# Another order for SP's loads and transposes in a fused attention and MLP kernel, with one matmul block moved on TensorE

## The chip, the cores and the metric

The kernel runs on one core of a Trainium2 chip. The metric is the device time of one execution in microseconds (us). Before the change it is 216.46 us, the median of four runs (215.32 to 217.26).

## The reference

Decayed linear attention over 4 batches, 8 heads, 768 positions and a head dimension of 64, in blocks of 64 positions with a running state, and then a layer norm with an MLP (512 to 2048 to 512) and a residual:

```python
for b in range(nb):                      # blocks of 64 positions
    intra = einsum('bhic,bhjc->bhij', qb, kb) * Dmask[None]
    intra = einsum('bhij,bhjd->bhid', intra, vb)
    inter = einsum('bhid,bhde->bhie', qb * lam_pow[None], kv_state)
    out[:, :, sl] = intra + inter
    kv_state = lam_block * kv_state + einsum('bhsd,bhse->bhde', kb * rev_pow, vb)
...
mu = mean(x); var = mean((x - mu) ** 2)
xn = (x - mu) / sqrt(var + 1e-06) * g_ln
out = x + maximum(xn @ w_ch1, 0.0) @ w_ch2
```

## The kernel before

The 4 x 768 rows are cut into 12 units of 256 positions, called pairs here (two chunks of 128), numbered u = 0 to 11; u goes over the batches first and then along the sequence, so pairs 0 to 3 start their sequences with no state. For each pair the kernel loads k, q and v (`load_one`, `load_window`, `fill`; lines 64 to 93) in float32 on SP's queue; rescales them to bf16 (`in_k` L199, `in_q` L210, `in_v` L216, the last giving the tile vb, mostly on GpSimd, called POOL); turns k and q by DMA transposes on SP (`transpose_dma`, L231, kq^T; for pairs 0 to 2 on TensorE, L224); computes k^T v (`kv`, L281, or `kv64`, L346), updates the state (`new_state`: a sum on VectorE, L291, and a decay on POOL, L287, or for a first state on ScalarE, L306), computes scores (`scores`, L247) and masks them on VectorE (`mask`, L257), multiplies them with v (`av`, L393) and adds the part from the state (`inter`, L406). `norm` (L428 to L435) gives xc, `to_xT` turns it into x^T (a DMA transpose on SP, L451, from pair 2 on), and `mlp` multiplies with both weights (L484 with ReLU L487; L522 with the residual L543), and the result is stored by SP (L550).

The order is written out by hand and nothing reorders it: each engine and each queue takes its instructions in the order in which the Python code issues them. Lines 588 to 695 do so for pairs 0 and 1 and begin pairs 2 to 4. Here `m1s(m1a, c, lo, hi)` issues the first-layer groups of pair 0 on weight chunk c, half a chunk (8 matmuls) at a time, `kv(1)` is the k^T v of pair 1, and `behind(tile)` makes POOL wait for a load before it issues more. From then on a list `plan` holds one MLP step each (8 matmuls of L484, or 4 of L522), and `add(n, ...)` puts steps of the attention behind the plan's step n: `p0(u)` converts the inputs of pair u, `s1(u)` to `s4(u)` do its attention, `p4(u)` issues its x^T, `transpose_dma` its kq^T, `load_one` one of its loads. Pairs from 6 on have another layout of the loads and the states (`X1`, `X2`, `X`).

The input tiles kin, qin and vin have three buffers each, so that the load of pair u takes the buffer of pair u - 3; vb has four; the PSUM tiles of the scores, tag "sc", have two. In `s1` the order on VectorE is: sum of the first state, mask of the first score tile, sum of the second state (which reads the first state after POOL has decayed it), mask of the second score tile; `s2` writes the next scores into the same two PSUM tiles. `make_keep64` builds a mask on POOL and copies half of it on VectorE (L142).

Of the kernel before, what the change touches and what calls it, by code (L numbers as in the profile page):

```python
# [16 lines left out]
def kernel(  # L17
# [11 lines left out]
    nc = tc.nc  # L29
# [38 lines left out]
    def fill(got, name, u, hs):  # L68
        src = dict(k=k, q=q, v=v)[name]
        if u < LB:  # L70
            nc.sync.dma_start(got[:, hs], source(src, u, hs))  # L71
            return
        cc, b = divmod(u, B)
        for j in range(2):
            nc.sync.dma_start(got[:, hs, j * D:(j + 1) * D],
                              src[b, hs, cc * W + j * C:cc * W + (j + 1) * C, :].rearrange("h p d -> p h d"))

    def load_one(u, name):
        got = inp.tile([128, H, 2 * D], F32, tag=name + "in", name=name + "in")
        fill(got, name, u, slice(0, H))  # L80
        qkv_in.setdefault(u, {})[name] = got.rearrange("p h (j d) -> p h j d", j=2)

    def load_window(u, after_pool=False, parts=1):
        got = {name: inp.tile([128, H, 2 * D], F32, tag=name + "in", name=name + "in") for name in "kqv"}
        if after_pool:

            nc.gpsimd.memset(got["k"][:, 0, 0:1], 0.0)
        n = H // parts
        order = [(name, i) for i in range(parts) for name in "kq"] + [("v", i) for i in range(parts)]
        for name, i in order:  # L90
            hs = slice(i * n, (i + 1) * n)
            fill(got[name], name, u, hs)
        qkv_in[u] = {name: f.rearrange("p h (j d) -> p h j d", j=2) for name, f in got.items()}
# [88 lines left out]
    def open_window(u):  # L182
        kq = wk.tile([128, 2, NP, 2, 2, D], BF16, tag="kq", bufs=3, name="kq")
        vb = wk.tile([128, H, 2, D], BF16, tag="vb", bufs=4, name="vb")
        st[u] = dict(kq=kq, vb=vb)
        if u < XB:
            st[u]["kqT"] = wk.tile([128, 2, NP, 2, 128], BF16, tag="kqT", bufs=3, name="kqT")
# [7 lines left out]
    def in_k(u, eng, hs=ALL):  # L195
        src = qkv_in[u]["k"][:, hs].rearrange("p (a e) j d -> p a e j d", e=2)
        dst = part(0, st[u]["kq"], hs)
        for j in range(2):
            (eng.copy if eng is nc.scalar else eng.tensor_copy)(dst[:, :, :, j], src[:, :, :, j])  # L199

    def in_q(u, eng, hs=ALL):
        src = qkv_in[u]["q"][:, hs].rearrange("p (a e) j d -> p a e j d", e=2)
        dst = part(1, st[u]["kq"], hs)
        if u < LB:
            lq = lam_q[:, hs, :].rearrange("p (a e) j -> p a e j", e=2)
        else:
            lq = lam_p[:, 0:1, hs].rearrange("p j (a e) -> p a e j", e=2).to_broadcast([128, (hs.stop - hs.start) // 2, 2, 2])
        n = (hs.stop - hs.start) // 2
        for j in range(2):
            eng.tensor_tensor(dst[:, :, :, j], src[:, :, :, j],  # L210
                              lq[:, :, :, j:j + 1].to_broadcast([128, n, 2, D]), op=ALU.mult)

    def in_v(u, eng, hs=ALL):
        n = hs.stop - hs.start
        lv = lam_v[:, hs, :, None] if u < LB else lam_p[:, 1, hs, None, None]
        eng.tensor_tensor(st[u]["vb"][:, hs], qkv_in[u]["v"][:, hs], lv.to_broadcast([128, n, 2, D]), op=ALU.mult)  # L216
# [36 lines left out]
    def mask(u, hf, heads=(0, 1)):  # L253
        s = st[u]
        kp = keep.rearrange("p a b t -> p a (b t)")
        for e in heads:
            nc.vector.tensor_tensor(s[f"mA{hf}"][:, e], s[f"sc{hf}"][e],  # L257
                                    kp[:, None, :, :].to_broadcast([128, 2, 2, 128]), op=ALU.mult)
# [11 lines left out]
    def kv(u, tag="mm"):  # L270

        s = st[u]
        cc, b = divmod(u, B)
        n_ab = 2 if (cc + 1) * W < S else 1
        bufs = dict(mm=4, sc=2, po=1)[tag]
        pk = [ps.tile([128, 2, NP, D], F32, tag=f"po{ab}" if tag == "po" else tag, bufs=bufs, name=f"pk{ab}")[:, 0] for ab in range(n_ab)]
        for p in range(NP):
            for j in range(2):
                for e in range(2):
                    for ab in range(n_ab):  # L280
                        nc.tensor.matmul(pk[ab][half[e], p, :], lhsT=s["kq"][half[ab], 0, p, j, e],  # L281
                                         rhs=s["vb"][half[ab], 2 * p + e, j],
                                         start=(p == 0 and j == 0), stop=(p == NP - 1 and j == 1), skip_group_check=True)
        s["pk"] = pk
# [9 lines left out]
    def new_state(u, ab, eng):  # L294

        s = st[u]
        b = u % B
        if ab == 1 and len(s["pk"]) == 1:
            return
        old = state.get(b)  # L300
        if ab == 0:
            s["S"] = [(old, old)]
        Sn = wk.tile([128, NP, D], BF16, tag="S", bufs=12, name="Sn")
        if old is None and eng is nc.scalar:
            for p in range(NP):
                nc.scalar.activation(Sn[:, p], s["pk"][ab][:, p], ACT.Identity, scale=lam_s[:, p:p + 1])  # L306
        elif old is None:
            decay(nc.vector, Sn, s["pk"][ab])
        else:
            tmp = s.pop("tmp", None) or state_sum(u, ab)  # L310
            decay(eng, Sn, tmp)
        state[b] = Sn
        if ab == 0:
            s["S"].append((Sn, Sn))
# [143 lines left out]
    def rstd_of(u):  # L458
        s = st[u]
        std = wk.tile([128, 2], F32, tag="std", name="std")  # L460
        nc.scalar.activation(std, s["mv"][:, :, 1], ACT.Sqrt, bias=eps_t)
        rstd = xp.tile([128, 2], F32, tag="rstd", name="rstd")
        nc.vector.reciprocal(rstd, std)
        x_keep[u] = (s["x"], rstd)
# [173 lines left out]
    m1a, m2a = mlp(0)  # L638
    m1b, m2b = mlp(1)

    def m1s(f, c, lo=0, hi=2):
        n = f.count // NWC
        for u in range(c * n + lo * n // 2, c * n + hi * n // 2):
            f(u)
# [17 lines left out]
    mask(1, 0)  # L662
    mask(1, 1)
    m1s(m1a, 1, 0, 1)
    kv(1, "sc")
    new_state(1, 0, nc.scalar)
    m1s(m1a, 1, 1, 2)
    rstd_of(0)
    m1s(m1a, 2, 0, 1)
    av(1, (0, 1))  # L670
# [21 lines left out]
    load_w2(3)  # L692
    in_v(2, nc.gpsimd)
    load_window(3, after_pool=True)
    load_window(4)

    def p0(u, k_eng=None):
        open_window(u)
        in_k(u, k_eng or nc.gpsimd)
        in_q(u, nc.gpsimd)  # L700
        in_v(u, nc.gpsimd)

    def s0(u):
        kv(u, "po")
# [138 lines left out]
    def add(at, *steps):  # L843
        after.setdefault(at, []).extend(steps)
# [6 lines left out]
    add(8, (s0, 2))  # L851
    add(10, (s3, 2))
    add(12, (s4, 2), (p4, 2), (p0, 3, nc.vector), (transpose_dma, 3))
    for n, name in zip((14, 15, 16), "kqv"):
        add(n, (load_one, 5, name))
    add(15, (rstd_of, 2))
    add(17, (p0, 4))
    add(25, (s1, 3))
    add(25, (transpose_dma, 4))
    add(27, (s2, 3))  # L860
    add(28, (p0, 5))
    add(29, (s3, 3))
    add(30, (s4, 3), (p4, 3))
    for n, name in zip((30, 31, 32), "kqv"):
        add(n, (load_one, 6, name))
    add(34, (rstd_of, 3), (make_keep64,))
    add(37, (transpose_dma, 5))
    add(38, (s1, 4))
    add(39, (p0, 6))
# [57 lines left out]
```

## Time and profile before

| | |
|---|---|
| median of four runs | 216.46 us |
| profiled execution | 216.34 us, of which the span is 214.4 us |
| TensorE matmul (PE) busy | 202.3 us, 94% of the span |
| VectorE (DVE), ScalarE (ACT), GpSimd (POOL) busy | 104.3, 87.2, 79.6 us |
| DMA moved | 37.13 MB, mean 173 GB/s |
| SP's DMA queue (q1) | 32.38 MB, 72.0% of 16 engines' span |

A line of a timeline gives the start in us from the start of the span, the duration in us, engine, line of the kernel, operation, what is written and read, the count, and in brackets how long the engine stood idle before it and what ended that. A line of the waits gives who waited for whom, us in total, how many times, and the longest. A line of a DMA issue ends with the us from the start of the issue to the landing of the data.

### The profile page before, as it was taken

The numbers are of one execution on the slowest core, as the hardware profiler recorded it, in microseconds if no ns is written. First come the engines' busy times: TensorE is split into PE (matmuls) and PEld (weight loads), VectorE is DVE, ScalarE is ACT, GpSimd is POOL, SyncE is SP. The second block draws the span as 40 slices with busy tenths as digits, with TensorE's granted clock in tenths as the row PEclk, the third lists the DMA queues.
The fourth block names the chain that finished last, engine by engine and source line by source line (L and its number), as shares of the span: only waits on it lengthen the run. The fifth ranks groups of instructions, "written<-read, shape, count | busy, mean of one in ns | idle before, by whom it ended". The sixth has DMA issues, their size and how long they took to land.

```text
span 214.4 us, 6657 instructions
## 1 busy us (share of the span) xinstructions
PE 202.3 (94%) x2899; PEld 138.2 (64%) x2899; DVE 104.3 (49%) x225; ACT 87.2 (41%) x165; POOL 79.6 (37%) x111
## 2 busy tenths in 40 slices
PE   2988799999999999999999999999999999999992
PEld 0467688544684675585585685784784874866861
DVE  2688380559268436747347256174183292522011
ACT  3865669220352244055163162361470460731600
POOL 4646339119656173229019137056074020000000
PEclk9999999999999999999999999999999999999999
DMA  4999999999999899999799799998998411320303
GB/s 114 295 272 210 202 279 145 225 275 274 196 305 243 168 210 167 114 215 211 134 228 191 146 235 185 191 213 179 208 244 133 117 28 28 99 52 0 98 3 95
DMA packets 94142, 37.13 MB, mean 173 GB/s; under 512 B 68385, under 2 KB 91169, under 8 KB 94114
## 3 DMA queue, kind: packets, MB, share of 16 engines
q1 hardware_dynamic: 89584, 32.38, 72.0%
q0 software_dynamic: 4224, 4.19, 12.4%
q8 instruction: 22, 0.36, 0.7%
q10 hardware_dynamic: 306, 0.14, 0.3%
q14 instruction: 6, 0.05, 0.1%
HBM read 27.27 MB, written 6.29 MB: 157 GB/s over the span
## 4 chain that ended last, share of the span: by engine, by line
PE 82%; DMA 8%; DVE 4%; SPq 3%; POOL 1%; issue 0%; ACT 0%; DVEq 0%
PE pm L484 37%; PE pm L522 34%; DMA vin<-in_v_dram 6%; SPq L71 3%; PE pm2h L513 2%; DMA xT<-xc 2%; PE po L393 2%; PE po L406 1%; PE sc L247 1%; DVE kq L199 1%; DVE xc L435 1%; PE po L380 1%; PE pk L281 1%; DVE stats L430 1%; POOL vb L216 1%; PE sc L327 1%
## 5 line engine op out<-in xcount | busy, mean ns | idle before, releaser
L487 ACT ACTIVATE hT<-pm 128x512 bf16<-128x512 f32 x92 | 55.0, 601 | 89.3 <-PE pm L484 89.1
L484 PE MATMUL pm<-xT,w 128*128 128x256 bf16 x736 | 86.1, 273 | 1.4 <-DMA w<-in_moe_w_ch_dram 0.9
L522 PE MATMUL pm<-w,hT 128*128 128x512 bf16 x368 | 82.3, 379 | 0.0
L484 PEld LDWEIGHTS <-w 128*128 128x128 bf16 x736 | 70.0, 98 | 13.0 <-DMA w<-in_moe_w_ch_dram 1.1
L522 PEld LDWEIGHTS <-hT 128*128 128x128 bf16 x368 | 35.5, 98 | 40.0
L543 DVE SCALAR_TENSOR_TENSOR o<-pm,rstd,x 128x512 f32<-128x512 f32 x23 | 17.1, 748 | 41.6 <-PE pm L522 41.4
L287 POOL TENSOR_TENSOR Sn<-Stmp,lam_s 128x256 bf16<-128x256 f32 x16 | 9.8, 614 | 69.1 <-DVE Stmp L365 49.0
L435 DVE SCALAR_TENSOR_TENSOR xc<-po,mv,g_row 128x512 bf16<-128x512 f32 (+1 forms) x24 | 16.8, 706 | 1.8
L257 DVE TENSOR_TENSOR mA<-sc,keep 128x512 bf16<-128x512 f32 x20 | 13.1, 684 | 6.5 <-PE sc L247 6.4
L428 ACT COPY x<-po 128x512 f32<-128x512 f32 x18 | 9.9, 589 | 11.3 <-PE po L393 5.5
L430 DVE BATCH_NORM_STATS2 stats<-x 128x6 f32<-128x512 f32 x18 | 12.4, 687 | 4.0 <-ACT x L428 3.9
L417 DVE COPY seen<-po 128x8 f32<-128x8 f32 x18 | 2.3, 162 | 23.1 <-PE po L406 23.1
L216 POOL TENSOR_TENSOR vb<-vin,lam_v 128x1024 bf16<-128x1024 f32 (+1 forms) x7 | 11.7, 1683 | 4.7 <-DMA vin<-in_v_dram 3.7
L210 POOL TENSOR_TENSOR kq<-qin,lam_q 128x512 bf16<-128x512 f32 x10 | 10.3, 1045 | 6.9 <-DMA qin<-in_q_dram 6.9
L210 POOL TENSOR_TENSOR kq<-qin,lam_p 128x512 bf16<-128x512 f32 x12 | 12.3, 1044 | 0.7 <-DMA qin<-in_q_dram 0.7
L216 POOL TENSOR_TENSOR vb<-vin,lam_p 128x1024 bf16<-128x1024 f32 x6 | 11.4, 1897 | 1.4 <-DMA vin<-in_v_dram 1.2
L199 POOL CAST kq<-kin 128x512 bf16<-128x512 f32 (+1 forms) x18 | 10.5, 611 | 0.6 <-DMA kin<-in_k_dram 0.6
L333 DVE TENSOR_TENSOR mA<-sc,keep 128x512 bf16<-128x512 f32 x12 | 8.2, 681 | 1.4 <-PE sc L327 1.4
L406 PE MATMUL po<-Sn,kqT 64*64 64x64 bf16 x216 | 7.4, 199 | 0.0
L224 PE MATMUL tp<-ident,kq 128*128 128x128 bf16 x48 | 6.1, 276 | 0.4 <-ACT kq L199 0.2
L224 PEld LDWEIGHTS <-kq 128*128 128x128 bf16 x48 | 4.1, 120 | 3.6 <-DVE kq L199 1.5
L406 PEld LDWEIGHTS <-kqT 64*64 64x64 bf16 x304 | 5.2, 108 | 1.5 <-issue 1.5
(98 smaller groups left out, 147.6 us busy)
## 6 DMA issues: line engine op xcount, KB each, us to landing
out_dram<-o SPq DMA_DIRECT2D x22, 256.0 KB, 4.9
w<-in_moe_w_ch_dram POOLq DMA_DIRECT2D x8, 512.0 KB, 10.2
kin<-in_k_dram SPq DMA_DIRECT2D x14, 256.0 KB, 3.7
qin<-in_q_dram SPq DMA_DIRECT2D x14, 256.0 KB, 4.9
vin<-in_v_dram SPq DMA_DIRECT2D x14, 256.0 KB, 5.7
kin<-in_k_dram SPq DMA_DIRECT2D x5, 512.0 KB, 8.1
qin<-in_q_dram SPq DMA_DIRECT2D x5, 512.0 KB, 8.6
vin<-in_v_dram SPq DMA_DIRECT2D x5, 512.0 KB, 6.9
```

Of the source, the lines that this page charges most:

```text
L199: (eng.copy if eng is nc.scalar else eng.tensor_copy)(dst[:, :, :, j], src[:, :, :, j])
L210: eng.tensor_tensor(dst[:, :, :, j], src[:, :, :, j], lq[:, :, :, j:j + 1].to_broadcast([128, n, 2, D]), op=ALU.mult)
L216: eng.tensor_tensor(st[u]["vb"][:, hs], qkv_in[u]["v"][:, hs], lv.to_broadcast([128, n, 2, D]), op=ALU.mult)
L224: nc.tensor.transpose(tp[:, i, j, :], s["kq"][:, a, p, j], ident)
L257: nc.vector.tensor_tensor(s[f"mA{hf}"][:, e], s[f"sc{hf}"][e], kp[:, None, :, :].to_broadcast([128, 2, 2, 128]), op=ALU.mult)
L406: nc.tensor.matmul(s["po"][ab][half[jq], 2 * p + e, :], lhsT=qT[half[e], p, jq, half[ab]], rhs=s["S"][ab][jq][half[e], p, :], start=False, ...
L430: nc.vector.bn_stats(stats, po if early else x)
L435: nc.vector.scalar_tensor_tensor(xc[:, sl], in0=po[:, sl], scalar=mv[:, 0:1], in1=g_row[:, sl], op0=ALU.subtract, op1=ALU.mult)
L484: nc.tensor.matmul(pm[:, b, :], lhsT=w1[n // W2K][:, kk, (n % W2K) * 128:(n % W2K + 1) * 128], rhs=xT_of[g][:, kk, 0:N], start=(b == 0 and ...
L487: nc.scalar.activation(hT[:, u * NB:(u + 1) * NB, 0:N], pm, ACT.Relu)
L522: nc.tensor.matmul(acc[i], lhsT=hT[:, kk, i * 128:(i + 1) * 128], rhs=w2[kk // W2K][:, kk % W2K, :], start=(kk == 0), stop=(kk == KB - 1))
L543: nc.vector.scalar_tensor_tensor(o[:, ab], in0=a, scalar=rstd[:, ab:ab + 1], in1=x[:, ab], op0=ALU.mult, op1=ALU.add)
```

## The change

Four things move; no operation is added or taken away.

1. `kv(1)` and the first state of pair 1 go behind the second half of the chunk-1 groups of pair 0's MLP.
2. The v load of pair 4 goes from ahead of pair 2's x^T to behind plan step 17, and that of pairs 5 and 6 to behind steps 31 and 38; the k and q loads of pair 5 go from 14 and 15 to 18 and 19, those of pair 6 from 30 and 31 to 32 and 33.
3. `in_v` of pairs 4, 5 and 6 leaves `p0` and stands at steps 26, 43 and 48; `p0(5)` goes from 28 to 31.
4. `transpose_dma` of pair 4 goes from 25 to 17.

```diff
     m1s(m1a, 1, 0, 1)
+    m1s(m1a, 1, 1, 2)
     kv(1, "sc")
     new_state(1, 0, nc.scalar)
-    m1s(m1a, 1, 1, 2)
     rstd_of(0)
...
     load_window(3, after_pool=True)
-    load_window(4)
+    load_one(4, "k")
+    load_one(4, "q")
 
     def p0(u, k_eng=None):
         open_window(u)
         in_k(u, k_eng or nc.gpsimd)
         in_q(u, nc.gpsimd)
-        in_v(u, nc.gpsimd)
+        if u not in (4, 5, 6):
+            in_v(u, nc.gpsimd)
...
-    for n, name in zip((14, 15, 16), "kqv"):
+    for n, name in zip((18, 19, 31), "kqv"):
         add(n, (load_one, 5, name))
     add(15, (rstd_of, 2))
-    add(17, (p0, 4))
+    add(17, (load_one, 4, "v"), (p0, 4), (transpose_dma, 4))
     add(25, (s1, 3))
-    add(25, (transpose_dma, 4))
     add(27, (s2, 3))
-    add(28, (p0, 5))
+    add(31, (p0, 5))
     add(29, (s3, 3))
     add(30, (s4, 3), (p4, 3))
-    for n, name in zip((30, 31, 32), "kqv"):
+    for n, name in zip((32, 33, 38), "kqv"):
         add(n, (load_one, 6, name))
     add(34, (rstd_of, 3), (make_keep64,))
+    for n, u in ((26, 4), (43, 5), (48, 6)):
+        add(n, (in_v, u, nc.gpsimd))
     add(37, (transpose_dma, 5))
```

## The prediction

> **What bounds the kernel now.** I read the page's shares first, then TensorE's waits, then the order of events around the two waits that the change is aimed at, then the queues that the change reorders.
>
> ```profile
> PE 202.3 (94%) x2899; PEld 138.2 (64%) x2899; DVE 104.3 (49%) x225; ACT 87.2 (41%) x165; POOL 79.6 (37%) x111
> PEclk9999999999999999999999999999999999999999
> PE pk L281 <- POOL vb L216: 1.3, 2, 1.1
> PE pm L484 <- DMA w<-in_moe_w_ch_dram: 0.9, 1, 0.9
> PE pm L484 <- DMA xT<-xc: 0.5, 1, 0.5
> ```
>
> TensorE (PE) is busy 202.3 of 214.4 us at a full granted clock. Its waits are short and early: the same view cut to 60 us and later lists none. A reordering that adds no work and takes none away can therefore win only the early waits, and lose wherever it makes a new one. The two that it touches are the 1.1 us of kv(1) for vb(1) and the 0.5 us of the second MLP stage (pair 2) for its x^T.
>
> **The first wait, in PE's timeline.** Columns: start us, us, operation, and in brackets the idle time before it.
>
> ```profile
> 21.49 1.05 PE L484 MATMUL pm<-xT,w 128*128 128x256 bf16 x8 [0.92 <-DMA w<-in_moe_w_ch_dram]
> 23.62 0.45 PE L281 MATMUL pk<-vb,kq 64*64 64x64 bf16 x32 [1.09 <-POOL vb L216]
> 24.00 1.92 PE L484 MATMUL pm<-xT,w 128*128 128x256 bf16 x16
> 21.68 1.90 POOL L216 TENSOR_TENSOR vb<-vin,lam_v 128x1024 bf16<-128x1024 f32 x1 [2.21 <-DMA vin<-in_v_dram]
> 24.06 0.19 POOL L579 CAST seen_p<-w 128x1 f32<-128x1 bf16 x1 [0.48 <-DMA w<-in_moe_w_ch_dram]
> w<-in_moe_w_ch_dram POOLq DMA_DIRECT2D x1, 512.0 KB, 11.3
> ```
>
> vb(1) is ready at 23.58 because v of pair 1 lands late; nothing in the change moves that. The 16 matmuls behind kv(1) are two groups: 8 on w1 chunk 1, which is there already, and 8 on chunk 2. The change puts the first 8 ahead of kv(1). On the chain 16 such matmuls took 1.85 us, so 8 take 0.92 us, and the wait of 1.09 shrinks to 0.17: **gain 0.92**. What becomes late next: the chunk-2 group now follows kv(1) at once, at 24.07. Chunk 2 was issued at 12.65 and took 11.3 (last line of the fence), so it landed at 23.95, 0.1 us early. Chunk 3, by the same view 17.91 + 8.6 = 26.5, is wanted at 27.84 - 0.92 = 26.92. The q part of pair 2 is done on POOL at 34.50 and its transposes, at 35.42 before, are wanted at 34.50. On ScalarE the moved group's ReLU now stands ahead of the four L306 copies of the state; it ends about 24.1, when kv(1) does, and the state, 0.93 us later, is still ahead of its reader at 25.65. Three covers of 0.0 to 0.4 us: bounds of the gain are 0 (all of them fail) and 1.09; I take 0.92, since each landing is read from a row.
>
> **The second wait.** SP's queue in order, and two landings (us from issue):
>
> ```profile
> 46.07 1.39 SPq L71 DMA_DIRECT2D qin<-in_q_dram  x1
> 47.51 1.76 SPq L71 DMA_DIRECT2D vin<-in_v_dram  x1
> 49.37 3.65 SPq L451 DMA_TRANSPOSE xT<-xc  x2
> 53.13 2.62 SPq L231 DMA_TRANSPOSE kqT<-kq  x2
> vin<-in_v_dram SPq DMA_DIRECT2D x1, 512.0 KB, 6.9
> xT<-xc SPq DMA_TRANSPOSE x1, 5.5
> ```
>
> v of pair 4 landed at 47.51 + 6.9 = 54.41; the first x^T of pair 2 at 49.37 + 5.5 = 54.87, the second at 51.83 + 3.5 = 55.3, and PE started at 55.43 after 0.53 of waiting. The x^T came 0.46 behind the v load. Without that load ahead, the transposes start as soon as SP has issued q (47.5) and the second xc is done (49.46 - 0.92 = 48.55), and their data wait only for q of pair 4. k of pair 4 landed at 42.81 + 8.1 = 50.9 and v at 54.41, so q is near 52.7 and the second x^T near 53.6. PE wants it at 55.43 - 0.53 - 0.92 = 53.98. **Gain 0.53**, bounds 0 and 0.53.
>
> The Trainium skill has a rule against counting this ("DMA: Bandwidth & Descriptors", section "Queues, rings and completion order"): descriptors of one issuing queue start in order, but completion need not be in that order. If transposes could overtake the v load, moving it would be worth 0 and the sum would end 0.53 us higher. The rows above show the x^T landing right behind the load, so I keep the gain.
>
> **What the moved loads cost.** No instruction is added: SP, POOL and PE issue as many as before. From 55 us on PE would run 0.92 + 0.53 = 1.45 us earlier. The new SP order is: x^T(2), kq^T(3), out(0), v(4), kq^T(4), k(5), q(5), out(1), x^T(3), v(5), k(6), q(6), out(2), kq^T(5), v(6), x^T(4); behind it all is as before. On POOL vb(4) goes behind the state of pair 3 (L287), vb(5) and vb(6) behind kq(6), and vb(6) stands directly ahead of the states of pair 5.
>
> The vb's own readers have room. v(4) is issued near 56.5 and lands with 6.3 to 6.9 us by 63.4; vb(4) takes 1.90 and is wanted at 72.90 - 1.45 = 71.4. v(5), issued near 69, lands near 75, and vb(5) is wanted at 84.7. Cost 0; without these 5 us and more of room it would be the lateness one for one.
>
> q(5) goes from 56.4 to between 59.1 and 62.7 (out 1.2 to 2.9, v 0.73, kq^T 2.6 to 4.6, k 0.57 from 53.8 on) and lands at 65.5 to 69.1 with the 6.4 us of its old issue. Its product takes 2.05, the keep64 masks behind it on POOL 0.9, and the copy of them on VectorE (L142) 0.2: done at 68.7 to 72.3. Behind that copy VectorE has L543 of the next tile (72.06 before, so 70.6 now) and then the first sum of pair 4 (73.33, so 71.9; L543 takes 0.75): the copy may end at 71.1. Cost 0 to 1.2; near the middle, 0.
>
> v(6) is the tight one. These rows are POOL's vb(6) and first state of pair 5, VectorE's last mask of the first scores of pair 5, and the chain's second scores that reuse the same PSUM tiles:
>
> ```profile
> 80.14 1.90 POOL L216 TENSOR_TENSOR vb<-vin,lam_p 128x1024 bf16<-128x1024 f32 x1 [0.72 <-DMA vin<-in_v_dram]
> 87.05 0.61 POOL L287 TENSOR_TENSOR Sn<-Stmp,lam_s 128x256 bf16<-128x256 f32 x1 [5.01 <-DVE Stmp L291]
> 88.04 0.68 DVE L257 TENSOR_TENSOR mA<-sc,keep 128x512 bf16<-128x512 f32 x1
> 89.41 0.35 PE sc L247 x16
> ```
>
> POOL idled 5 us between the first two; vb(6) moves into that hole. From the state's start to the mask's end is 88.72 - 87.05 = 1.67 us (the second L291 sum on VectorE waits for the state, and the mask stands behind that sum). PE wants the tiles at 89.41 - 1.45 = 87.96, so vb(6) must end at 86.3 and v(6) must land by **84.4**. When does it land? SP resumes at 70.36 - 1.45 = 68.9; then v(5) 0.73, k(6) 1.20, q(6) 1.81, out(2) 1.39, kq^T(5) 4.61 bring it to 78.6; v(6)'s second half goes out about 1.3 later, at 79.9, and lands 4.0 us (80.1 - 76.08, its old second half) to 5.6 us later: 83.9 to 85.5. With both kq^T issues at their short time (2.6 together) it is 81.9. If the DMA engines set the pace, which moved the same work from 70.36 to the landing of kq^T(5) at 85.5 in 15.1 us, v(5) adds 2.2 (its old landing at 66.4 came that long after the store ahead of it) and it is 86.2. Cost 0 to 1.8; I take the middle of the two landings, 84.7, so **0.3**. It would become a wait of PE's second scores for VectorE.
>
> **Sum.** The profiled execution took 216.34 us (span 214.4 and 1.94 around it): 216.34 - 0.92 - 0.53 + 0.3 = 215.2. The median of the runs is 0.12 above that execution: **215.3**.
>
> **Rivals.**
> - Half of it: x^T(2) is still not ahead of PE, or the chunk-2 and chunk-3 covers fail. For it: covers of 0.1 and 0.4 us. Against: the landings come from rows. Either gain alone leaves 216.46 - 0.92 = 215.5 or 216.46 - 0.53 = 215.9.
> - Slower: v(6) late holds POOL, and through the state, VectorE and the PSUM tiles, PE at the second scores of pair 5. It decides from a landing at 84.4, and eats the whole gain at 84.4 + 1.45 = 85.85. For it: the DMA engines are near full from 44 to 84 us, and the work-bound landing of 86.2. Against: k(6) and q(6) no longer wait behind anything else, and POOL has 5 us of hole. At 86.2 the time is 216.46 - 1.45 + 1.8 = 216.8; if q(5) too is at its late end, 218.0.
> - More than the sum: in the timed runs the early waits are longer than in the profile, so that more than 1.45 goes; with 0.4 more (half of the 0.8 between the median and the highest run) and everything in reach it is 216.46 - 1.8 - 0.4 = 214.3. Against: only 1.09 + 0.53 + 0.18 (the x^T of pair 1, L455) of PE's waits are in reach, 1.8 in all.
>
> **How the numbers follow.** Forecast (214.6 to 215.8) 0.52; half of it 0.16; slower than before 0.24, of which 0.09 beyond 1%; more than the sum 0.08. One per cent is 2.16 us, about what a measurement of this kernel can tell from no change: faster by over that needs a time under 214.3 and thus more than the reachable waits, 0.07; slower by over that needs 218.6, with v(6), q(5) and another cover failing together, 0.09; the rest 0.84. The range runs from 214.3 (everything reachable) to 217.1 (v(6) at its work-bound landing and a little of q(5)); the forecast's own is 214.6 to 215.8.
>
> **What would show it.** Right: PE's wait at kv(1) near 0.2 us, no wait for x^T at the stage that started at 55.43, that start near 54.0, and v(6) landing near 84.7. Wrong: a wait of L484 for w near 24 or 27 us, or idle PE at L247 near 88 us behind VectorE's masks, with POOL's vb(6) ending after 86.3; VectorE's L142 copy after 71.1 would show the q(5) price. A PE gap anywhere after 95 us would be something that I have not seen.

## The result and the profile after

The changed kernel takes 217.72 us (median of 42 runs, 216.36 to 221.19) where the kernel before takes 216.77 (63 runs). The ratio of the two is 1.007, with a 95% interval of 1.0051 to 1.0088: 1.1 to 1.9 us slower (the medians over all runs differ by 0.95 us). The forecast was 215.3 us, 1.2 us faster than before, with a range up to 217.1. The profiled execution took 217.31 us with a span of 215.6, 1.2 us more span than before. All ratios here come from fast runs alone, and the first profiles of `kv_only` (mean granted clock 0.676) and `after_late_stores` (span 705.9 us) are slow executions that are not used.

Names with a number in brackets belong to that pair: v(6) is the load of v of pair 6, vb(6) its conversion, kq^T(5) and x^T(3) are DMA transposes, out(1) is the store of pair 1's result, and kv(6) or kv64(6) the k^T v of pair 6. Times "in the chain" are from the chain of work that ended last, which follows each step back to what released it.

The page's shares and clock, and the list of TensorE's (PE's) waits, of the kernel after:

```profile
PE 202.6 (94%) x2899; PEld 138.2 (64%) x2899; DVE 104.4 (48%) x225; ACT 87.2 (40%) x165; POOL 79.6 (37%) x111
PEclk9999999999999999999999999999999999999999
PE sc L247 <- DVE mA L257: 1.4, 1, 1.4
PE pm L484 <- DMA xT<-xc: 1.0, 1, 1.0
PE pm L484 <- DMA w<-in_moe_w_ch_dram: 0.9, 2, 0.7
PE pk L281 <- POOL vb L216: 0.3, 1, 0.3
```

The work is the same to 0.3 us and the clock is full. The two early waits are gone (the 0.3 left at L281 is that of pair 0), and two stand there that the first profile of the kernel before did not have. PE's timeline shows both early gains and both losses in their places:

```profile
21.37 1.92 PE L484 MATMUL pm<-xT,w 128*128 128x256 bf16 x16 [0.69 <-DMA w<-in_moe_w_ch_dram]
23.22 0.45 PE L281 MATMUL pk<-vb,kq 64*64 64x64 bf16 x32
23.88 1.05 PE L484 MATMUL pm<-xT,w 128*128 128x256 bf16 x8 [0.22 <-DMA w<-in_moe_w_ch_dram]
71.51 1.03 PE L484 MATMUL pm<-xT,w 128*128 128x256 bf16 x8 [1.03 <-DMA xT<-xc]
90.67 0.41 PE L247 MATMUL sc<-kqT 64*64 64x128 bf16 x15 [1.42 <-DVE mA L257]
```

A ledger of the same instructions before and after: the second MLP stage starts at 54.08 in the chain instead of 55.43 (1.35 gained); the third (x^T(3)) at 71.51 instead of 71.86 (0.35 left); behind the second scores of pair 5, kv64(6) runs at 94.59 in the chain instead of 93.25 (1.34 lost, so 1.69 went between the two, of which 1.42 is idle time). From there on both kernels run without a wait, and the last step starts 1.24 later (211.73 against 210.49).

SP's queue after, from the loads of pair 5 to v(6), and two landings (us from issue): the first x^T of pair 3 and the second half of v(6).

```profile
61.67 0.58 SPq L71 DMA_DIRECT2D kin<-in_k_dram  x1
62.30 1.51 SPq L71 DMA_DIRECT2D qin<-in_q_dram  x1
63.91 1.64 SPq L550 DMA_DIRECT2D out_dram<-o  x2
65.66 3.45 SPq L451 DMA_TRANSPOSE xT<-xc  x2
69.17 0.58 SPq L71 DMA_DIRECT2D vin<-in_v_dram  x1
69.80 1.96 SPq L75 DMA_DIRECT2D kin<-in_k_dram  x2
71.80 2.58 SPq L75 DMA_DIRECT2D qin<-in_q_dram  x2
74.48 3.27 SPq L550 DMA_DIRECT2D out_dram<-o  x2
77.91 4.32 SPq L231 DMA_TRANSPOSE kqT<-kq  x2
82.28 1.21 SPq L75 DMA_DIRECT2D vin<-in_v_dram  x2
xT<-xc SPq DMA_TRANSPOSE x1, 5.4
vin<-in_v_dram SPq DMA_DIRECT2D x1, 256.0 KB, 4.1
```

In the kernel before, x^T(3), the start of the third stage and v(6) read:

```profile
67.80 2.51 SPq L451 DMA_TRANSPOSE xT<-xc  x2
71.86 1.04 PE L484 MATMUL pm<-xT,w 128*128 128x256 bf16 x8
73.47 3.67 SPq L75 DMA_DIRECT2D vin<-in_v_dram  x2
```

The two x^T(3) transposes go out at 65.66 and 67.90, more than a microsecond before those of the kernel before (67.80 and 69.09), yet the first needs 5.4 us to land instead of 2.4 (71.1 instead of 70.2), and the second lands at 67.90 + 3.5 = 71.4. Before, PE came at 71.86 and found both there. For the second the trace has no landing; with the 2.4 us of the first, 69.09 + 2.4, it is estimated at 71.5, so that x^T(3) had some 0.4 us to spare, and landed no later after the change than before. Now PE is 1.35 us ahead and waits. Then v(6) goes out at 82.28 and 82.91 and lands at 87.0. What that does is read from POOL's timeline:

```profile
87.09 1.90 POOL L216 TENSOR_TENSOR vb<-vin,lam_p 128x1024 bf16<-128x1024 f32 x1 [4.81 <-DMA vin<-in_v_dram]
88.95 0.61 POOL L287 TENSOR_TENSOR Sn<-Stmp,lam_s 128x256 bf16<-128x256 f32 x1
```

and from VectorE's, in the same stretch:

```profile
89.60 0.42 DVE L291 TENSOR_TENSOR Stmp<-pk,Sn 128x256 f32<-128x256 f32 x1 [2.36 <-POOL Sn L287]
89.94 0.68 DVE L257 TENSOR_TENSOR mA<-sc,keep 128x512 bf16<-128x512 f32 x1
```

POOL stands 4.81 us at vb(6), which nobody wants before kv64(6); the state of pair 5 behind it starts at 88.95 instead of 87.05, VectorE's second sum waits 2.36 for it, the mask behind that sum ends at 90.6, and PE, which has written only the first of its 16 scores, goes on at 90.67.

### The profile page after: what moved, and what is told of

Its sections match the earlier page's. It is cut to its first block, busy times and chain, and to the rows that moved or that the text cites. A ratio compares the mean times of both kernels' runs of the same rounds, so it can differ in the third digit from the quotient of the medians.

```text
span 215.6 us, 6656 instructions
## 1 busy us (share of the span) xinstructions
PE 202.6 (94%) x2899; PEld 138.2 (64%) x2899; DVE 104.4 (48%) x225; ACT 87.2 (40%) x165; POOL 79.6 (37%) x111
## 4 chain that ended last, share of the span: by engine, by line
PE 75%; DMA 13%; SPq 5%; POOL 3%; DVE 3%; issue 1%; POOLq 0%
PE pm L484 33%; PE pm L522 32%; DMA w<-in_moe_w_ch_dram 5%; DMA qin<-in_q_dram 3%; DMA kin<-in_k_dram 3%; SPq L71 2%; DMA vin<-in_v_dram 2%; PE pm2h L513 2%; PE po L406 1%; PE po L393 1%; SPq L75 1%; PE po L380 1%; POOL kq L210 1%; POOL vb L216 1%; PE sc L327 1%; PE sc L247 1%
## 5 line engine op out<-in xcount | busy, mean ns | idle before, releaser
L224 PE MATMUL tp<-ident,kq 128*128 128x128 bf16 x48 | 6.4, 277 | 0.5 <-ACT kq L199 0.2
L224 PEld LDWEIGHTS <-kq 128*128 128x128 bf16 x48 | 4.1, 120 | 3.9 <-DVE kq L199 1.5
```

The costliest lines, as they stand in the source:

```text
L224: nc.tensor.transpose(tp[:, i, j, :], s["kq"][:, a, p, j], ident)
```

## The experiments

Theory: the early gains are real; they are given back at two places, where SP's order and POOL's order make new waits. Rival theories: the gains were never there; or it is not the order but the amount of transfers between 55 and 90 us that sets the landings, so that every order only chooses which reader waits.

### One part at a time

`kv_only` is the kernel before with part 1 of the change alone:

```diff
     m1s(m1a, 1, 0, 1)
+    m1s(m1a, 1, 1, 2)
     kv(1, "sc")
     new_state(1, 0, nc.scalar)
-    m1s(m1a, 1, 1, 2)
```

> The kernel before with only the move of kv(1) behind the second chunk-1 group. Theory (the early gain is real and is given back later in SP's and POOL's order): PE's wait at kv(1) falls from 1.1 to 0.3 us, a wait of 0.1 to 0.3 for weight chunk 2 appears, and nothing later takes it back: 0.7 to 0.9 us faster than before, ratio about 0.996. Rival (an earlier PE only meets the same late x^T of pair 2, whose landing is set by the DMA queue): the wait for x^T(2) grows from 0.5 to about 1.3 and the time is that of before, ratio 1.000.

Measured: ratio 1.003 (0.9981 to 1.0079), which settles nothing. The same kernel again:

> The kernel before with only the move of kv(1), once more, since its first timing (ratio 1.003, interval 0.998 to 1.008) settles nothing. Theory: PE's wait at kv(1) near 0.2 to 0.3 us, no later wait grown by more than 0.3, ratio 0.995 to 0.998. Rival (the wait only goes to x^T(2), which the v load ahead of it holds): PE's wait for x^T(2) near 1.3 us, ratio 1.000 to 1.002.

Measured: ratio 1.0021 (0.999 to 1.0052); no gain. PE's timeline shows where it goes:

```profile
23.54 1.05 PE L484 MATMUL pm<-xT,w 128*128 128x256 bf16 x8 [0.24 <-DMA w<-in_moe_w_ch_dram]
55.26 3.65 PE L484 MATMUL pm<-xT,w 128*128 128x256 bf16 x32 [1.13 <-DMA xT<-xc]
72.32 1.03 PE L484 MATMUL pm<-xT,w 128*128 128x256 bf16 x8 [0.48 <-DMA xT<-xc]
```

The rival was right: PE is early at 24 us, and the second stage still starts at 55.26 (before: 55.43), because x^T(2) lands at 55.1, 0.9 us behind v(4) as in the kernel before. Part 1 alone shows no gain; its time can come through only where x^T(2) lands earlier too.

`sp_only` is the changed kernel with `kv(1)` back in its old place.

> The changed kernel with kv(1) back in its old place. Theory: the waits at x^T(3) and at the second scores of pair 5 are set by landings of DMA transfers, so PE arriving 0.7 us later waits about that much less; the time is within 0.3 us of the changed kernel's, ratio to before 1.005 to 1.008. Rival (the loss comes with the kv(1) move): no slower than before, ratio 0.997 to 1.000.

Measured: ratio 1.010 (1.0033 to 1.0168). As the theory had it, though above its 1.005 to 1.008, the loss is in the parts 2 to 4 and not in the move of kv(1): no slowing at all, the rival, lies outside the interval.

`kv_and_v4` is the kernel before with part 1 and a single load moved:

```diff
-    load_window(4)
+    load_one(4, "k")
+    load_one(4, "q")
...
-    add(12, (s4, 2), (p4, 2), (p0, 3, nc.vector), (transpose_dma, 3))
+    add(12, (s4, 2), (p4, 2), (p0, 3, nc.vector), (transpose_dma, 3), (load_one, 4, "v"))
```

> The kernel before with the move of kv(1) and one load alone in another place: v of pair 4 directly behind x^T(2) and kq^T(3). No other load, transpose or conversion moves. Theory (the two early gains are real, and the losses come from the moved k and q of pair 5 and v of pair 6): both early waits gone, no wait at x^T(3) above 0.3 and none at pair 5's scores above 0.3; 1.2 to 1.5 us faster than before, ratio 0.993 to 0.995. Rival (any early gain is lost again at x^T(3), because the DMA queue has no time to give): PE's wait for x^T(3) takes 0.8 to 1.0 us, ratio 0.998 to 1.000.

Measured: ratio 1.0018 (0.9982 to 1.0053), with a wait of 1.6 us at x^T(3). The theory failed here, and the wait is where its rival had it, though larger than the rival's 0.8 to 1.0: with none of the moved loads of pairs 5 and 6, the gain is lost at x^T(3) all the same, one v load further down the same queue. The transposes go out at 69.43 and 70.72, 1.6 us later than in the kernel before, so here they are late outright and do not only meet an earlier PE. In this profile PE also waited 1.0 us at L224 near 19 us, ahead of all that the edit moves, and began kv(3) only 0.35 us earlier than before (58.67 instead of 59.02).

### The two repairs

`vb6_behind_states` changes only POOL's order in the changed kernel:

```diff
-    for n, u in ((26, 4), (43, 5), (48, 6)):
+    for n, u in ((26, 4), (43, 5)):
         add(n, (in_v, u, nc.gpsimd))
...
-    add(50, (s1, 5), (rstd_of, 4))
+    add(50, (s1, 5), (in_v, 6, nc.gpsimd), (rstd_of, 4))
```

> The changed kernel with vb(6) on POOL behind the two states of pair 5 instead of ahead of them; SP's order untouched. Theory (POOL, held by the late v(6), holds the state, VectorE's sum and mask, and PE): the state starts near 86.7, PE's wait of 1.4 us at the second scores of pair 5 is gone, 1.4 us faster than the changed kernel, ratio to before about 1.000. Rival (v(6) is late for whatever reads it): the wait only moves to kv64(6), which wants vb(6) near 91 to 93 us; the time stays at that of the changed kernel.

Measured: ratio to before 1.0015 (0.9981 to 1.0048), so about 1.2 us (217.72 - 1.0015/1.007 x 217.72) faster than the changed kernel, and no wait of L247 in PE's list. POOL's timeline:

```profile
86.73 0.61 POOL L287 TENSOR_TENSOR Sn<-Stmp,lam_s 128x256 bf16<-128x256 f32 x1 [4.13 <-DVE Stmp L291]
87.88 0.61 POOL L287 TENSOR_TENSOR Sn<-Stmp,lam_s 128x256 bf16<-128x256 f32 x1 [0.54 <-DVE Stmp L291]
88.45 1.90 POOL L216 TENSOR_TENSOR vb<-vin,lam_p 128x1024 bf16<-128x1024 f32 x1
```

SP's order is that of the changed kernel and v(6) is as late as ever (landed at 87.3); only the instruction that stands in front of the state has changed, and the wait of 1.4 is gone. That shows the last link of the loss: POOL's order. A wait of 0.4 at x^T(4), behind v(6) on SP's queue, is what appears next.

`kq5_early` puts the k and q loads of pair 5 back to steps 14 and 15 (`zip((14, 15, 31), "kqv")`).

> The changed kernel with the loads of k and q of pair 5 back at steps 14 and 15, ahead of out(0), v(4) and kq^T(4). Theory (x^T(3) lands late because the k, q and out transfers stand directly ahead of it on SP's queue): x^T(3) lands near 70, PE's wait of 1.0 us for it is gone; with the wait at pair 5's scores growing by as much if v(6) lands no earlier, the time improves by 0 to 1.0 us on the changed kernel, ratio to before 1.003 to 1.007. Rival (the queue is full whichever order it has): x^T(3) still lands near 71.4 and PE still waits 0.8 to 1.0 us for it.

Measured: ratio 1.0061 (1.0021 to 1.0101). In its profile x^T(3) lands at 68.9 and is not waited for, and PE begins kv(5) at 83.83 instead of 85.72; 0.5 of these 1.9 us it had already at kv(3). But vb(6) starts only 1.35 earlier (85.74 instead of 87.09), and the wait at pair 5's second scores is 1.9 instead of 1.4. The interval holds the changed kernel's 1.007, so no gain on it shows; what was won at x^T(3) went for the most part into the next late landing, as the theory had it. `both_mended` has both repairs.

> The changed kernel with both repairs: k and q of pair 5 back at steps 14 and 15, and vb(6) on POOL behind the states of pair 5. Theory: neither the wait at x^T(3) nor that at pair 5's scores; the two early gains stay: 1.0 to 1.4 us faster than before, ratio 0.994 to 0.996. Rival (with v(6) still late, x^T(4) behind it on SP's queue, or kv64(6), becomes the next wait): 0.4 to 1.0 us of PE's wait at x^T(4) near 88 us, ratio 0.997 to 1.000.

Measured: ratio 0.9984 (0.9943 to 1.0024), no different from before. With the same SP order as `kq5_early` up to v(6), its profile has 1.2 us of wait at x^T(3) and 0.7 at x^T(4). So moving k and q of pair 5 is no sure cure for x^T(3): one profile without the wait, one with it. `v6_early` moves the v(6) load ahead of out(2) and kq^T(5) instead (`zip((32, 33, 34), "kqv")`).

> The changed kernel with the load of v of pair 6 moved from step 38 to step 34, ahead of out(2) and kq^T(5) on SP's queue; POOL's order is untouched. Theory (vb(6) holds POOL only because v(6) lands late): v(6) lands near 82 us, vb(6) is done before the state of pair 5 is due, the 1.4 us at pair 5's second scores is gone, ratio about 1.000 to 1.002, with the wait at x^T(3) still there. Rival (kq^T(5) is then late in its place): a new wait of PE at the first scores of pair 5 near 85 us, ratio 1.003 or more.

Measured: ratio 1.0008 (0.9972 to 1.0044). The wait for the mask is gone, and in its place are 0.9 us at the first scores of pair 5, for kq^T(5), as the rival had it, beside 1.3 at x^T(3) (up to 90 us the granted clock of this execution was 1.00). The time is that of the theory (1.000 to 1.002), not the rival's 1.003 or more; v(6) landed at 83.6 where the theory said 82.

### Less on the queue

Every order so far had lost the gain at another reader. The next kernels take transfers out of the stretch instead: the stores of pairs 0 to 2 (512 KB each) go on SP's queue far behind it, and o gets six buffers.

```diff
-        o_of[u] = wk.tile([128, 2, DM], F32, tag="o", bufs=3, name="o")
+        o_of[u] = wk.tile([128, 2, DM], F32, tag="o", bufs=6, name="o")
...
-    elif ab == 1:
-        for j in range(2):
-            nc.sync.dma_start(rows[j], o[half[j]])
+    elif ab == 1 and u > 2:
+        store(u)
...
+    for n, u in ((126, 0), (130, 1), (134, 2)):
+        add(n, (store, u))
```

> The changed kernel with the stores of pairs 0 to 2 (1.5 MB) taken out of the stretch up to 85 us and issued on SP at steps 126, 130 and 134 (o has six buffers for it); all other orders as in the changed kernel. Theory (from 55 to 90 us SP's queue and the DMA engines have no time to spare, so every reordering only chooses which reader waits): without these transfers x^T(3) and v(6) land early enough; PE's waits of 1.0 at x^T(3) and 1.4 at pair 5's scores are gone and 2.0 to 2.5 us of the changed kernel's time with them, ratio to before 0.993 to 0.997. Rival (it is the order of SP's instructions, each held by its own semaphore, and not the amount of transfers): v(6) still lands near 87, the waits stay, ratio 1.004 to 1.008.

Measured: ratio to before 0.9975 (0.9942 to 1.0007), 2.1 us less than the changed kernel (1.007 - 0.9975 of 216.77). Its profile was taken again:

> The changed kernel with the stores of pairs 0 to 2 postponed, for a profile with a full clock. Theory: no wait at x^T(3) above 0.3 us, v(6) landed by 84 and no wait at pair 5's second scores above 0.3; perhaps 1 us at kq^T(11), as with the same stores in the other kernel. Rival: both waits there as in the changed kernel (1.0 and 1.4).

Measured: PE waits neither at x^T(3) nor at pair 5's scores; SP has issued q(5) by 61.6 and stands idle until x^T(3) at 67.81. Each half of x^T(3) lands 2.4 us after its issue, where the changed kernel's took 5.4 and 3.5; q(5), the last transfer ahead of it, had landed at 66.6. But PE came late in this execution: kv(3) began at 59.97 instead of 57.50, after 2.0 us of waiting for vb(1) and with a granted clock of 0.94 over the first 30 us. That it did not wait at x^T(3) therefore proves little by itself. v(6) landed only at 86.2, against an expected 84, and PE came to the second scores at 90.06, 1 us later than in the changed kernel; whether that place would have held against an early PE this profile does not say. The time, 2.1 us less, fits both. `late_stores` is the kernel before with the same stores postponed.

> The kernel before with the same three stores postponed and nothing else. Theory: before has no wait of PE behind 60 us, and its early waits (vb(1), w, x^T(2)) lie ahead of the first store, so nothing changes: ratio 0.998 to 1.001. Rival (the queue also costs the kernel before something that no wait shows): ratio below 0.997.

Measured: ratio 1.0026 (0.9989 to 1.0063). Postponing alone brings no gain that the timing shows. A second profile,

> late_stores, unchanged, for a second profile. If the landing of v(1) belongs to the program, vb(1) starts at 19.4 again with no wait at kv(1). If it belongs to the execution, any start from 19.3 to 22.9, and 21 or later in about half of such looks, with 1 us or more of wait at kv(1).

shows vb(1) starting at 19.36, as in the first (19.35), with no wait at kv(1) in either, as if the landing of v(1) belonged to the program. It also shows 1.2 us at L327 for kq^T(11), beside which the postponed stores stand. `kv_v4_late_stores` joins them with `kv_and_v4`:

> The kernel before with kv(1) moved, v of pair 4 behind x^T(2) and kq^T(3), and the three stores postponed. Theory: both early waits are gone and x^T(3), whose queue is 1 MB shorter, lands before PE wants it; PE has no wait above 0.3 us behind 45 us; 1.0 to 1.5 us faster than before, ratio 0.993 to 0.996. Rival (the early part is set by the landings of v(1), w and q(2), which differ from execution to execution, and the two early gains are mostly not there in most of them): ratio 0.997 to 1.000.

Measured: ratio 0.9962 (0.9929 to 0.9995), with 1.0 us of wait at kq^T(11) near 169 us. `kv_v4_later_stores` moves the stores out of its way, to steps 139, 142 and 145:

> As kv_v4_late_stores (kv(1) moved, v of pair 4 behind x^T(2) and kq^T(3), stores of pairs 0 to 2 postponed), but with those stores at steps 139, 142 and 145 instead of 126, 130 and 134. Theory (at 126 to 134 they stood around kq^T(11) on SP's queue and made PE wait 1.0 us for it near 169): that wait is gone, ratio to before 0.990 to 0.994. Rival (the stores then only delay x^T(11), behind step 151): a new wait of 0.5 to 1.0 us near 186 us, ratio 0.995 to 0.998.

Measured: 215.08 us, ratio 0.9935 (0.9896 to 0.9975): faster than both kernels. The waits of its profile:

```profile
PE pk L281 <- POOL vb L216: 1.6, 1, 1.6
PE pm L484 <- DMA w<-in_moe_w_ch_dram: 0.5, 1, 0.5
PE pm L484 <- DMA xT<-xc: 0.3, 1, 0.3
```

PE is busy for 29.96 of the 30 us from 60 to 90, as in the kernel before (29.96), where `after_look` below has 28.18. The x^T(3) transposes go out at 66.27 and 67.90, where `kv_and_v4` had 69.43 and 70.72, and land at 69.5 and 70.3, 0.8 us ahead of PE, which comes at 71.15. In this execution kv(1) waited 1.6 us for vb(1), and its time, 217.15 us, is above the median, so the profile does not show the whole gain.

The same two early edits that were worth nothing in `kv_and_v4` come with a time 1.4 us below that of before once x^T(3) has 1 MB less in front of it. The later steps without the two early edits were not run.

### The same kernels profiled again

The first gain hangs on when v(1) lands, so the kernels themselves were profiled again.

> The kernel before, unchanged, for a second profile. If the 1.1 us of kv(1) for vb(1) is a property of the order, it is there again within 0.3. If it is a property of that one execution (v(1) landed 13.7 us after its issue), it can be anything from 0 to 1.1, with the wait for weight chunk 2 or x^T(2) larger instead, and the span within 1 us of the first profile's.

Measured: vb(1) starts at 21.77, kv(1) waits 1.37, within 0.3 of the first profile.

> The kernel before, unchanged, a third profile. If the landing of v(1) differs between executions of one kernel, vb(1) may start near 19.4 with no wait at kv(1), and then x^T(2) is waited for longer (about 1.1 us more), since its landing does not follow; if it is the same in each, 21.7 and 1.1 to 1.4 again.

Measured: 21.48 and 1.11. The first of these two profiles has 0.3 us of wait for x^T(2), the second 0.5 for x^T(3): even the kernel before has no slack there in some executions.

> The changed kernel, unchanged, once more. The waits at x^T(3) and at pair 5's second scores are there again, 0.5 to 1.5 and 1.0 to 2.0 us, whichever time v(1) lands at: earlier PE, larger waits.

Measured: 21.61; 1.3 at x^T(3) and 1.3 at pair 5's second scores, so both losses are there again, with a span of 216.1.

> sp_only, unchanged, for a second profile. If the landing of v(1) belongs to the program, vb(1) starts at 19.5 again and kv(1), here in its old place, does not wait. If it belongs to the execution, 21 or later in about half of such looks. In both cases waits of 0.3 to 1.4 us at x^T(3) and of 1.0 to 2.0 at pair 5's second scores.

Measured: 21.61, where the first profile of the same kernel had 19.53 and no wait at kv(1); the wait at kv(1) is 1.1 now, and the late waits are 1.7 and 1.4.

## Why the prediction was wrong, point by point

- **The first wait: right.** Chunk 2 became the next wait (0.22, where 0.1 of cover was read), and the multiplication with v behind it (L393) started at 24.86 instead of 25.85, 0.99 earlier. But alone it shows no gain (`kv_only_2`).
- **The second wait: right**, x^T(2) landing at 49.99 + 3.5 = 53.5 against a predicted 53.6. Both together gave 1.35 of the predicted 1.45 at 54 us. With v(4) ahead x^T(2) landed 0.5 and 0.9 us behind it (54.8 and 55.3 after 54.4), and with v(4) gone it landed 1.8 us earlier: had the transposes overtaken the load, moving it would have brought nothing. The overtaking that the Trainium skill ("DMA: Bandwidth & Descriptors", section "Queues, rings and completion order") leaves open did not show here.
- **x^T(3): a step that is missing from the sum.** The prediction listed it in SP's new order and costed v(4), v(5), q(5) and v(6), but not the transposes whose neighbours changed. PE was to come to the third MLP stage 1.45 us earlier, so x^T(3) had to land about a microsecond earlier too, and in the new order k(5), q(5) and out(1) went out directly ahead of it. Its second half landed at 71.4, and PE waited 1.03. In the changed kernel this wait is hidden behind the next one, since PE's restart at 90.67 is set by v(6); it decides once v(6) is out of the way, as in `vb6_behind_states`, where 0.8 of it stays and the gain does not come back.
- **v(6): the right mechanism with the wrong size, and the term that turned the sum.** The prediction named it as the slower rival, with POOL, the state, the second sum, the mask and the PSUM tiles, and 84.4 as the landing from which it decides; the forecast took a landing of 84.7 and 0.3 us. It landed at 87.0. By the prediction's own rule that costs 2.6 us instead of 0.3, and its sum becomes 216.46 - 1.45 + 2.6 = 217.6, against 217.72 measured. PE stood 1.03 of these 2.6 us at x^T(3) and 1.42 at the second scores. `vb6_behind_states` shows that the link to PE is POOL's order.
- **What made v(6) late** is SP's way to it. Resumption at 68.9 was nearly right (69.17), but k(6), q(6) and out(2), taken at 1.20, 1.81 and 1.39 us from the rows before, took 1.96, 2.58 and 3.27, 3.4 us more in all. Before, SP needed 8.42 us from k(6) at 70.36 to kq^T(5) at 78.78, and 3.67 of these stood in the row of v(6); the prediction took them out and put 0.73 in for v(5). After, with v(5) in place of v(6), as many bytes, it needed 8.74 (69.17 to 77.91). So the time did not go with the row that was moved. That a full queue holds SP back is read from this and not tested by itself. The profile's chain puts the second half of kq^T(5) down to POOL's conversion of q(6), which ended at 80.4; but kq^T(5) reads the conversion of pair 5, done at 70.8. The bound from the DMA engines' pace (86.2) was the nearer one, and the sum took the middle below it.
- **q(5):** L142 ended at 71.86, later than the 71.1 that was said to be harmless, and cost nothing: PE, held by x^T(3), came to kv(4) only at 72.47, and VectorE's sum behind L142 still stood idle for 0.32 us until then. Without the wait at x^T(3) it could have cost something, so this was luck.
- **The rest:** no PE gap behind 95 us in the changed kernel, as forecast. The chance of 0.24 for slower than before was built on v(6) and q(5); x^T(3), which in `kv_and_v4` eats the gain without a late v(6), was in none of the rivals.

What stays open: how much of the 1.4 us of the best version each of its edits brings, and at what landing of v(6) the wait at pair 5 returns when the stores are late.

## What to carry to other kernels

When an order on a full queue is changed, list every transfer whose neighbours change and write its landing beside the moment that its reader will want it once the expected gain has come true; the slack in the profile before is the most that can be won until that landing moves too. The issue time of a DMA in a trace is no fixed price of the instruction: in the changed kernel the two halves of out(2), 256 KB each, took 2.62 and 0.60 us, and the first half of x^T(3) took 1.20 us before the change and 2.14 after it. A row from one order is therefore a poor price for the same row in another. And put a conversion that waits for a late load behind the work that somebody is waiting for, on in-order engines: here that one line of order was worth about 1.2 us.

## What was not expected of the hardware

v(1) is issued at about 7.9 us on SP in every kernel, and no instruction up to 20 us differs between them, yet vb(1), which needs it, started anywhere from 19.3 to 22.9 us; in `sp_only` at 19.53 in one profile and 21.61 in the other, and POOL waited for the load in the second alone. With it the wait at kv(1) comes and goes by up to 2.0 us, so the gain of part 1 is not in every execution, though all three profiles of the kernel before had the wait (1.1 to 1.4). The program may have a share in it: the three of the kernel before lie within 0.3 us of each other, and the two of `late_stores` within 0.01. The weight loads that POOL issues run beside v(1) at that time. The Trainium skill ("DMA: Bandwidth & Descriptors", section "Queues, rings and completion order") says that each DMA engine serves its queues in turn, packet by packet; that would let the two queues share the engines differently from one execution to the next, which no run here shows. The traces speak against a mere exchange between the two: the weight chunk issued at 11.8 us landed 8.6 us later in `late_stores`, where v(1) was early, and 9.6 us later in the kernel before, where it was late, so both came early together. What makes the difference stays open.
